# A fused attention and MLP kernel: q and k turned by VectorE in 32x32 blocks in place of DMA transposes, from the eighth group on

## The chip, the cores and the metric

One Trainium2 chip, of which the kernel uses one core. The metric is device time in microseconds (us), lower is better. The kernel before the change takes 414.19 us, the median of three runs (412.75 to 414.78). One of its executions was profiled; where a duration stands below, it comes from that execution. Engines are named as the profile names them: PE is TensorE's matmul, PEld its weight load, DVE is VectorE, ACT is ScalarE, POOL is GpSimd, and SP is SyncE, which here only issues DMAs.

## The reference

An attention over 8 batches of 12 heads, 448 rows of 64 columns each, with q and k normed by their root mean square, is followed by a two-layer MLP with a leaky activation:

```python
def rmsnorm(x, g):
    rms = np.sqrt(np.mean(x * x, axis=-1, keepdims=True) + 1e-06)
    return x / rms * g
q_n, k_n = (rmsnorm(q, g_q), rmsnorm(k, g_k))
scores = (1.0 / np.sqrt(64)) * np.matmul(q_n, k_n.transpose(0, 1, 3, 2))
scores = scores - np.max(scores, axis=-1, keepdims=True)
attn = np.exp(scores)
attn = attn / (np.sum(attn, axis=-1, keepdims=True) + 1e-09)
attn_out = np.matmul(attn, v)                      # (8, 12, 448, 64)

x = attn_out.transpose(0, 2, 1, 3).reshape(8 * 448, 12 * 64)
h = x @ w_in                                       # (3584, 768) @ (768, 2048)
g = np.maximum(h, 0.0) + alpha * np.minimum(h, 0.0)
out = g @ w_out                                    # (3584, 2048) @ (2048, 768)
```

## The kernel before

**Groups and bursts.** The work on q and k goes in 24 groups `y` of four heads, three groups to a batch. `TD` is 7: groups 0 to 6 are prepared in one way, groups 7 to 23, "from the eighth on", in another; it is the second way that the change replaces. A group has seven tiles `j` of keys. The program is a list of 69 bursts `n`. A burst issues two to four score tiles (`score`, PE, L357) with their exponentials (`soft`, ACT, L371), sums and products with v where they are due, and then the MLP units planned for it: `up` (first layer, PE L496, then ACT L536, then DVE L540), `down` (second layer), or `quad_a`, `quad_b`, `quad_c` (the second layer of two token tiles in seven products of half size in place of eight, L623). Each engine works through its instructions in the order of the program, which is written out by hand and by a small planner; nothing is reordered later.

**Preparing a group y >= 7.** `load_qk` loads q and k in two DMAs from SP's queue (L126), 128 partitions by 896 values, two head-halves of 64 partitions each. POOL squares them (`square`, L177), DVE sums each row of 64 (`reduce`, L185), ACT takes the logarithm and then the exponential of -0.5 times it (`root`, L195 and L196), POOL multiplies the rows by the result and writes them as fp16 (`scale`, L205), two DMA transposes put the 64 columns of each head on the partitions (`turn_dma`, L304), and DVE multiplies k in place by the product of the two gains (`turn`, L315). The scores of the group then read `qT` and `kT`.

**Order and places.** `root_at[y]` is the burst that holds `root` and `scale` of group y, `turn_at[y]` the burst that holds the gain product; in between the DMA transposes run by themselves. The roots of groups 7 to 23 stand in bursts 17, 20, 22, 24, 28, 29, 32, 36, 37, 40, 44, 45, 48, 52, 53, 56, 60, and their gain products in bursts 19, 23, 25, 27, 31, 33, 35, 39, 41, 43, 47, 49, 51, 55, 57, 59, 63. Within a burst the order is: scores and the first exponentials, sums and products, `root` and `scale` (L1116 to L1128), `turn_dma`, the load of a later group (L1132), and then the units of the burst with other small work (`jobs`) handed out between them, one after every second `up`. So ACT's logarithm of a root stands in ACT's queue ahead of the first `up` of its burst.

**Banks.** PSUM has two banks for scores (`pss`), two for everything of the MLP and half of the products with v (`psf`, tag `mm`: `hT`, `op`, `qx`, `qz`, `qc`, `avb`, `dnb`), and one pair (`psa`, tag `acc`) that the sums `dn`, the products `av` and now and then a spare MLP unit (`hTa`, `opa`, `qza`) take in turn. An `up` needs 1.14 us of PE; its bank is free again when ACT L536 (0.63 us) and then DVE L540 (0.62 us) have read it.

**Buffers.** `nat` (what is loaded) has four, `qs` (scaled rows) two, that is one group, `qT` and `kT` three each, `rden` (denominators) two. Groups 2, 5 and 8 are loaded into a piece of `arena`, which holds mixed weights later.

Of the kernel before, what the change touches and what calls it, by code (L numbers as in the profile page):

```python
# [21 lines left out]
def kernel(  # L22
# [17 lines left out]
    J = S // 64  # L40
    HH = H // 2
# [70 lines left out]
    def load_qk(y, hold=False):  # L112
        b, i = divmod(y, G)
        for nm in "qk":
            if y in (2, 5, 8):
                t = lent(HB + "qk".index(nm) * NB4, NB4).rearrange(
                    "p (h j d) -> p h j d", h=2, j=J
                )
            else:
                t = ld.tile([128, 2, J, D], FP32, name="nat", tag="nat", bufs=4)  # L120
            if hold and nm == "q":

                nc.scalar.copy(out=t[:, 0, 0, 0:1], in_=expb)
            o = t.rearrange("p h j d -> p h (j d)")
            for h in range(2) if (y, nm) == (0, "q") else (slice(0, 2),):
                nc.sync.dma_start(out=o[:, h], in_=SRC[nm][b, :, ds(2 * i, 2)][:, h])  # L126
            nat[y, nm] = t

# [34 lines left out]
    def square(y, nm):  # L163
        src = nat[y, nm].rearrange("p h j d -> p (h j d)")
        if y % 2 and y < 3 * G + 1:
            sq = lent(HB + (2 + "qk".index(nm)) * NB4, NB4).rearrange("p (n d) -> p n d", d=D)
        else:
            sq = ld.tile([128, 2 * J, D], FP32, name="sq", tag="sq", bufs=2)
        sqf = sq.rearrange("p n d -> p (n d)")
        if (y, nm) == (1, "q"):  # L170
            nc.scalar.activation(out=sqf, in_=src, func=AF.Square)
        else:

            n = 2 if (y, nm) in ((2, "q"), (G, "k")) else 1
            for h in range(n):
                c = ts(h, 2 * J * D // n)
                nc.gpsimd.tensor_mul(out=sqf[:, c], in0=src[:, c], in1=src[:, c])  # L177
        sqs[y, nm] = sq

    def reduce(y, nm, heads=None):  # L180
        if y not in ss_t:
            ss_t[y] = ld.tile([128, 2, 2, J], FP32, name="ss", tag="ss", bufs=4)
        o = ss_t[y][:, "qk".index(nm)].rearrange("p h j -> p (h j)").unsqueeze(2)
        for c in [slice(0, 2 * J)] if heads is None else [ts(h, J) for h in heads]:
            nc.vector.tensor_reduce(  # L185
                out=o[:, c], in_=sqs[y, nm][:, c], axis=AXIS_X, op=ALU.add
            )

    def root(y, nms="qk"):
        n = len(nms)  # L190
        at = "qk".index(nms[0])
        if at == 0:
            rr_t[y] = ld.tile([128, 2, 2, J], FP32, name="rr", tag="rr", bufs=4)
        rr, ss = rr_t[y][:, ds(at, n)], ss_t[y][:, ds(at, n)]
        nc.scalar.activation(out=rr, in_=ss, func=AF.Ln, scale=1.0 / D, bias=RMS_EPS)  # L195
        nc.scalar.activation(out=rr, in_=rr, func=AF.Exp, scale=-0.5)  # L196

    def scale(y, nm):
        if y in (1, 3, 5):
# [15 lines left out]
    def part_square(nm, h, j, eng):  # L215
        if ("sq", nm) not in tops:
            tops["sq", nm] = ld.tile([128, 2 * J, D], FP32, name="sq", tag="sq", bufs=2)
        o = tops["sq", nm].rearrange("p (h j) d -> p h j d", h=2)[:, h, j]
# [6 lines left out]
    def part_reduce(nm, h, j):  # L225
        if 0 not in ss_t:
            ss_t[0] = ld.tile([128, 2, 2, J], FP32, name="ss", tag="ss", bufs=4)
        nc.vector.tensor_reduce(
            out=ss_t[0][:, "qk".index(nm), h, j].unsqueeze(3),
            in_=tops["sq", nm].rearrange("p (h j) d -> p h j d", h=2)[:, h, j],  # L230
# [3 lines left out]
    def part_root(nm, j):  # L234
        if 0 not in rr_t:
            rr_t[0] = ld.tile([128, 2, 2, J], FP32, name="rr", tag="rr", bufs=4)
# [23 lines left out]
    def part_copy(nm, j, eng):  # L260
        if (0, nm) not in qkT:
            qkT[0, nm] = att.tile([128, J, 2, 64], FP16, name=f"{nm}T", tag=f"{nm}T", bufs=3)
# [18 lines left out]
    def turn_one(y, nm):  # L281
# [6 lines left out]
        t = att.tile([128, J, 2, 64], FP16, name=f"{nm}T", tag=f"{nm}T", bufs=3)  # L288
# [12 lines left out]
    def turn_dma(y):  # L301
        for nm in "qk":
            t = att.tile([128, J, 2, 64], FP16, name=f"{nm}T", tag=f"{nm}T", bufs=3)
            nc.sync.dma_start(  # L304
                out=t.rearrange("p j g c -> p j (g c)"),
                in_=qs[y, nm].rearrange("p j h d -> p (j h d)"),
                transpose=True,
            )
            qkT[y, nm] = t

    def turn(y):
# [21 lines left out]
        for tp, nm in zip(tps, "qk"):  # L333
            t = att.tile([128, J, 2, 64], FP16, name=f"{nm}T", tag=f"{nm}T", bufs=3)
# [84 lines left out]
    def den_pre(ys):  # L419
        accs = [psf.tile([128, 512], FP32, name="dnb", tag="mm") for _ in range(2)]  # L420
        ones_over(accs, ys)
        r = att.tile([128, 2, S], FP32, name="rden", tag="rden")[:, :, : cols_of(ys)]
# [8 lines left out]
    def log(ys):  # L431
        n = cols_of(ys)
        r = att.tile([128, 2, S], FP32, name="rden", tag="rden")[:, :, :n]
# [120 lines left out]
    def down(tile, oh, jobs=(), spare=False):  # L554
# [10 lines left out]
        for f, a in jobs:  # L565
            if f is not turn:
                f(*a)
        o = result()
        nc.vector.tensor_copy(out=o, in_=op[:, :OH])
        for f, a in jobs:  # L570
            if f is turn:
                f(*a)
# [472 lines left out]
    for n in range(NB):  # L1045
# [70 lines left out]
        if n in roots:  # L1116
            y = roots[n]
            work = [(root, (y,)), (scale, (y, "q")), (scale, (y, "k"))]
# [10 lines left out]
            if y >= TD:  # L1129
                turn_dma(y)  # L1130
# [22 lines left out]
        if ups_first and n in dens and not lead:  # L1153
            for f, a in jobs.pop(n, ()):
                f(*a)
        turned = n in turns and gaps[n] and (turns[n] >= TD or turns[n] <= 2 * G)
# [73 lines left out]
```

## Time and profile before

| what | profile of before |
|---|---|
| the profiled execution, device time | 414.78 us |
| its span, first to last instruction | 413.0 us |
| bytes moved by DMA | 53.38 MB, 129 GB/s on average |
| DMA packets under 512 bytes | 34880 of 67330 |
| PE idle, 46 to 90 us | 1.92 us |
| PE idle, 90 to 165 us | 0.07 us |
| PE idle, 165 to 330 us | 2.01 us |
| PE idle, 330 to 413 us | 4.19 us |
| POOL waiting for a load before a square, 90 to 330 us | 25.3 us in 6 waits |
| POOL waiting for a DMA transpose to free `qs` | 4.3 us in 3 waits |
| mean granted TensorE clock | 0.995 |

The profiled execution lies 0.6 us above the median of the three runs. The busy share of an engine is the time in which it executed something, over the span. A wait is put down to what ended it. The idle times of PE are 44, 75, 165 and 83 us less PE's busy time in these four stretches; the first group that is changed is loaded at 46.6 us, and the last one's gain product is at 328 us, so the second to fourth rows from the end of that list frame the part of the run that the change touches.

### The profile page before, as it was taken

Reading aid. Unit: us, or ns where it says so; the run is one execution under the profiler, and the core shown is the slowest. Engines: PE = TensorE matmul, PEld = TensorE weight load, DVE = VectorE, ACT = ScalarE, POOL = GpSimd, SP = SyncE. Lnnn points to the kernel's source line nnn. Section 1 sums busy time; section 2 is a strip of 40 time slices with the busy share of each in tenths; the row PEclk is TensorE's granted clock in tenths of the full one; section 3 lists DMA queues with packets and bytes.
Section 4 is the critical chain, followed back from the end, with each engine's and each line's share of the span. In section 5 each row is a group of like instructions: output and inputs, shape, how many; then the busy total and the mean of one; then the engine's idle time right before and its main releaser. Section 6 shows DMA issues by size and latency. Waiting matters only on the chain.

```text
span 413.0 us, 11724 instructions
## 1 busy us (share of the span) xinstructions
PE 398.9 (97%) x5055; PEld 208.1 (50%) x5055; DVE 266.9 (65%) x420; ACT 257.3 (62%) x390; POOL 255.8 (62%) x184
## 2 busy tenths in 40 slices
PE   7889999899999999999999999999999999999996
PEld 3344445444456445554455445545555455645664
DVE  3876875476567388785688585958576755465322
ACT  5697787567846785557766786875657783135110
POOL 5599996589677969376373847484724407300870
PEclk9899999999999999999999999999999999999999
DMA  8999899957754894329861697279332700320143
GB/s 259 231 217 206 172 200 155 248 169 103 163 81 134 204 169 91 115 63 197 144 168 48 173 138 177 63 180 193 59 75 54 127 3 24 75 59 0 30 103 97
DMA packets 67330, 53.38 MB, mean 129 GB/s; under 512 B 34880, under 2 KB 66768, under 8 KB 67280
## 3 DMA queue, kind: packets, MB, share of 16 engines
q1 hardware_dynamic: 53344, 40.45, 40.5%
q0 software_dynamic: 13536, 11.81, 21.5%
q8 instruction: 39, 0.64, 0.7%
q10 hardware_dynamic: 400, 0.39, 0.3%
q14 instruction: 11, 0.09, 0.1%
HBM read 45.62 MB, written 11.01 MB: 137 GB/s over the span
## 4 chain that ended last, share of the span: by engine, by line
PE 49%; DVE 6%; ACT 0%; issue 0%; DVEq 0%
PE hT L496 14%; PE hTa L496 7%; PE qx L623 5%; PE sc L357 3%; PE oq L623 3%; PE qc L623 3%; PE qz L623 2%; PE av L382 2%; PE oqm L623 2%; PE avb L382 1%; PE dn L382 1%; PE oqa L623 1%; DVE ss L185 1%; DVE xT L481 1%; DVE kT L315 1%; PE qza L623 1%
## 5 line engine op out<-in xcount | busy, mean ns | idle before, releaser
L371 ACT ACTIVATE expT<-sc 128x896 f16<-128x896 f32 x168 | 147.8, 913 | 55.4 <-PE sc L357 55.0
L496 PE MATMUL hT<-xT,w_in_sb 128*128 128x448 f16 x546 | 113.7, 353 | 0.4 <-DVE gT L540 0.2
L496 PEld LDWEIGHTS <-w_in_sb 128*128 128x128 f16 x768 | 72.7, 98 | 74.8 <-issue 10.1
L540 DVE TENSOR_TENSOR gT<-hT,gT 128x448 f16<-128x448 f32 x91 | 56.6, 623 | 40.1 <-ACT gT L536 39.2
L205 POOL TENSOR_TENSOR qs<-nat,rr 128x896 f16<-128x896 f32 x36 | 60.9, 1713 | 33.4 <-issue 24.9
L536 ACT ACTIVATE gT<-hT,cols 128x448 f16<-128x448 f32 x90 | 56.9, 633 | 33.9 <-PE hT L496 33.7
L177 POOL TENSOR_TENSOR sq<-nat 128x896 f32<-128x896 f32 x32 | 53.1, 1681 | 38.0 <-DMA nat<-in_q_dram 25.3
L357 PE MATMUL sc<-qT,kT 64*32 64x448 f16 (+1 forms) x1092 | 53.3, 358 | 3.5 <-ACT expT L371 1.1
L623 PEld LDWEIGHTS <-gT 128*128 128x128 f16 x352 | 33.4, 98 | 26.0 <-issue 4.9
L496 PE MATMUL hTa<-xT,w_in_sb 128*128 128x448 f16 x210 | 45.4, 352 | 0.0
L185 DVE TENSOR_REDUCE ss<-sq 128x14 f32<-128x896 f32 (+1 forms) x37 | 38.3, 1052 | 0.6 <-POOL sq L177 0.6
L481 DVE TENSOR_TENSOR xT<-av,rden 64x448 f16<-64x448 f32 (+1 forms) x37 | 27.2, 734 | 13.5 <-PE av L382 5.5
L536 ACT ACTIVATE gT<-hTa,cols 128x448 f16<-128x448 f32 x35 | 22.2, 635 | 19.1 <-PE hTa L496 19.1
L540 DVE TENSOR_TENSOR gT<-hTa,gT 128x448 f16<-128x448 f32 x35 | 21.8, 624 | 17.7 <-ACT gT L536 17.6
L357 PEld LDWEIGHTS <-kT 64*32 64x32 f16 (+1 forms) x1092 | 15.6, 93 | 34.7 <-issue 29.3
L558 PE MATMUL op<-w_out_sb,gT 128*128 128x384 f16 x160 | 27.4, 326 | 0.0
L382 PEld LDWEIGHTS <-vt 64*32 64x32 f16 x1344 | 20.2, 92 | 14.1 <-issue 5.0
L611 POOL TENSOR_TENSOR gs<-gT 128x1024 f16<-128x1024 f16 x3 | 6.4, 2121 | 30.3 <-DVE gT L540 28.1
L558 PEld LDWEIGHTS <-gT 128*128 128x128 f16 x192 | 18.0, 98 | 13.5 <-issue 2.4
L382 PE MATMUL av<-expT,vt 64*32 64x448 f16 x896 | 24.3, 350 | 0.3 <-DVE osb L671 0.3
L619 POOL TENSOR_TENSOR gT<-gT 128x1024 f16<-128x1024 f16 x11 | 23.8, 2166 | 0.0
L623 PE MATMUL qx<-w_out_sb,gT 128*128 128x384 f16 x120 | 20.9, 326 | 0.0
(148 smaller groups left out, 494.1 us busy)
## 6 DMA issues: line engine op xcount, KB each, us to landing
out_dram<-osb SPq DMA_DIRECT2D x107, 96.0 KB, 2.8
nat<-in_k_dram SPq DMA_DIRECT2D x21, 448.0 KB, 5.4
nat<-in_q_dram SPq DMA_DIRECT2D x20, 448.0 KB, 4.9
vt<-in_v_dram POOLq DMA_DIRECT2D x8, 672.0 KB, 11.0
w_in_sb<-in_moe_w_in_dram POOLq DMA_DIRECT2D x24, 128.0 KB, 5.0
w_out_sb<-in_moe_w_out_dram POOLq DMA_DIRECT2D x4, 768.0 KB, 10.8
arena<-in_q_dram SPq DMA_DIRECT2D x3, 448.0 KB, 7.8
arena<-in_k_dram SPq DMA_DIRECT2D x3, 448.0 KB, 8.5
```

The costliest lines, as they stand in the source:

```text
L177: nc.gpsimd.tensor_mul(out=sqf[:, c], in0=src[:, c], in1=src[:, c])
L185: nc.vector.tensor_reduce(out=o[:, c], in_=sqs[y, nm][:, c], axis=AXIS_X, op=ALU.add)
L205: eng.tensor_mul(out=t.rearrange("p j h d -> p h j d"), in0=nat[y, nm], in1=rr_t[y][:, "qk".index(nm)].unsqueeze(3).broadcast_to((128, 2, ...
L357: nc.tensor.matmul(out=sc[ds(64 * g + m * c, m), par, :S].rearrange("p (j c) -> p j c", j=J), lhsT=kT[ds(64 * par, 64), j, g, ts(c, m)], r ...
L371: nc.scalar.activation(out=expT[y][:, j], in_=scs[y, j][:, :, :S], func=AF.Exp, scale=QK_SCALE, bias=EXP_BIAS,)
L382: nc.tensor.matmul(out=accs[g][ds(32 * n, 32), :S], lhsT=weights(g, y, par, c, j), rhs=expT[y][ds(64 * g, 64), j, par, :], start=(j == 0), ...
L481: nc.vector.tensor_mul(out=x, in0=av, in1=r)
L496: nc.tensor.matmul(out=hT[:, :S], lhsT=w_in_sb[:, block_of(g, i), ts(ft, 128)], rhs=xT[b][:, g, i, :], start=(i == 0 and g == 0), stop=(i ...
L536: nc.scalar.activation(out=g, in_=hT[:, :S], func=AF.Copy, scale=alpha_sb[:, ft : ft + 1])
L540: nc.vector.tensor_max(out=g, in0=hT[:, :S], in1=g)
L558: nc.tensor.matmul(out=op[:, :OH], lhsT=gT[:, ft, ts(tile % J, 128)], rhs=w_out_sb[:, ft, ts(oh, OH)], start=(ft == 0), stop=(ft == NF - 1),)
L623: nc.tensor.matmul(out=bank[:, c], lhsT=g[:, ft], rhs=v[:, ft, c], start=(first and ft == 0), stop=(ft == HF - 1), skip_group_check=True,)
```

## The change

For groups 7 to 23 each row of q and k is loaded twice: partition quarters 0 and 2 hold it from column 0 on, quarters 1 and 3 from column 32 on, 32 tokens times 14 rows and two heads in each quarter. A tile is then 128 x 28 slots of 64 values, of which the first 32 are used; the squares are written over the second 32. Four DMAs per tensor take the place of one. A row's 64 squares now lie in two quarters, so each quarter's sums are half sums: `fold` swaps them between neighbouring quarters by four copies and adds. `scale` writes the fp16 rows so that the values of two neighbouring rows lie side by side as one 4-byte word, and `flip` turns 32x32 blocks of such words on DVE straight into `qT` and `kT`. `turn_dma` is gone; the gain product stays. The buffers are cut to make room: `nat` is twice as wide, `sq` is gone, `qT` and `kT` have two instead of three, `rden` one instead of two, `ss` and `rr` three instead of four. In groups 0 to 6 only the places of the squares change.

A `flip` pair stands one burst ahead of the gain product, among the jobs. But `qs` holds one group, so where the next group's root comes in that same burst or earlier, the pair is issued right in front of that root. By the bursts given above that is so for the flips of groups 8, 9, 11, 12, 14, 15, 17, 18, 20 and 21; those of 7, 10, 13, 16, 19, 22 and 23 are jobs.

```diff
@@ def load_qk
-            if y in (2, 5, 8):
-                t = lent(HB + "qk".index(nm) * NB4, NB4).rearrange(
-                    "p (h j d) -> p h j d", h=2, j=J
-                )
+            n = "qk".index(nm)
+            if y == 8:
+                t = lent(HB + 2 * n * NB4, 2 * NB4)
+            elif y in (2, 5):
+                t = lent(HB + n * NB4, NB4)
             else:
-                t = ld.tile([128, 2, J, D], FP32, name="nat", tag="nat", bufs=4)
+                t = ld.tile([128, 4 * J * D], FP32, name="nat", tag="nat", bufs=4)
+            if y >= TD:
+                load_twice(y, nm, t.rearrange("p (g t d) -> p g t d", g=2, d=D))
+                continue
...
+    def load_twice(y, nm, t):
+        b, i = divmod(y, G)
+        n = 2 * J * D - HD
+        for par in range(2):
+            src = FULL[nm][b, ds(4 * i + 2 * par, 2)].rearrange(
+                "g (p t) d -> p g (t d)", p=32
+            )
+            for e in range(2):
+                nc.sync.dma_start(
+                    out=t[ds(64 * par + 32 * e, 32)].rearrange("p g t d -> p g (t d)")[:, :, :n],
+                    in_=src[:, :, ds(HD * e, n)],
+                )
+        nat[y, nm] = t.rearrange("p g t d -> p (g t) d")
@@ def square
+        if y >= TD:
+            t = nat[y, nm]
+            sqs[y, nm] = t[:, :, HD:]
+            nc.gpsimd.tensor_mul(out=sqs[y, nm], in0=t[:, :, :HD], in1=t[:, :, :HD])
+            return
...
@@ def reduce
+        if y >= TD:
+            nc.vector.tensor_reduce(
+                out=ss_t[y][:, "qk".index(nm)].rearrange("p g h j -> p (g h j)").unsqueeze(2),
+                in_=sqs[y, nm], axis=AXIS_X, op=ALU.add,
+            )
+            return
...
+    def fold(y):
+        o = ld.tile([128, 4 * 2 * J], FP32, name="sf", tag="sf", bufs=1)
+        ss = ss_t[y].rearrange("p n g h j -> p (n g h j)")
+        for n in range(4):
+            nc.vector.tensor_copy(out=o[ds(32 * (n ^ 1), 32)], in_=ss[ds(32 * n, 32)])
+        nc.vector.tensor_add(out=ss, in0=ss, in1=o)
@@ def root
+        if y >= TD:
+            fold(y)
@@ def scale
+        if y >= TD:
+            t = ld.tile([128, J, HD, 4], FP16, name="qs", tag="qs", bufs=2)
+            r = rr_t[y][:, "qk".index(nm)].rearrange("p g h j -> p (g h) j")
+            nc.gpsimd.tensor_mul(
+                out=t.rearrange("p j d n -> p n j d"),
+                in0=nat[y, nm][:, :, :HD].rearrange("p (n j) d -> p n j d", j=J),
+                in1=r.unsqueeze(3).broadcast_to((128, 4, J, HD)),
+            )
+            qs[y, nm] = t.rearrange("p j d n -> p (j d n)").bitcast(FP32)
+            return
@@
-    def turn_dma(y):
-        for nm in "qk":
-            t = att.tile([128, J, 2, 64], FP16, name=f"{nm}T", tag=f"{nm}T", bufs=3)
-            nc.sync.dma_start(
-                out=t.rearrange("p j g c -> p j (g c)"),
-                in_=qs[y, nm].rearrange("p j h d -> p (j h d)"),
-                transpose=True,
-            )
-            qkT[y, nm] = t
+    def flip(y, nm):
+        t = att.tile([128, J, 2, 64], FP16, name=f"{nm}T", tag=f"{nm}T", bufs=2)
+        nc.vector.transpose(
+            out=t.rearrange("p j g c -> p (j g c)").bitcast(FP32).rearrange(
+                "p (j g c) -> p j g c", j=J, g=2
+            ),
+            in_=qs[y, nm].rearrange("p (j d g) -> p j g d", j=J, g=2),
+        )
+        qkT[y, nm] = t
...
@@ def down
-            if f is not turn:
+            if f not in (turn, flip):
...
@@ the list of bursts
         if n in roots:
             y = roots[n]
+            for nm in "qk" if y > TD and (y - 1, "q") not in qkT else "":
+                flip(y - 1, nm)
             work = [(root, (y,)), (scale, (y, "q")), (scale, (y, "k"))]
...
-            if y >= TD:
-                turn_dma(y)
...
+        flips = [(flip, (turns[n + 1], nm)) for nm in "qk"] if turns.get(n + 1, 0) >= TD else []
+        if flips and flips[0][1] not in qkT:
+            jobs.setdefault(n, []).extend(flips)
```

## The prediction

> **What bounds the kernel now.** I read the busy times first, then four stretches, the waits of PE and POOL, the DMA issues, and last the order of time around the roots. From the page, the windows (columns: PE, PEld, DVE, ACT, POOL busy, granted clock, DMA share, GB/s) and the issues:
>
> ```profile
> PE 398.9 (97%) x5055; PEld 208.1 (50%) x5055; DVE 266.9 (65%) x420; ACT 257.3 (62%) x390; POOL 255.8 (62%) x184
> ...
> 90.00:165.00 75.00, 74.93 (x872) 38.35 (x878) 48.56 (x74) 51.59 (x80) 62.82 (x39) 1.00 0.63 129
> 165.00:330.00 165.00, 162.99 (x2351) 84.71 (x2336) 121.31 (x193) 114.15 (x171) 92.23 (x55) 1.00 0.65 124
> ...
> nat<-in_k_dram SPq DMA_DIRECT2D x21, 448.0 KB, 5.4
> ...
> kT<-qs SPq DMA_TRANSPOSE x17, 3.7
> ```
>
> PE is the bound, and has next to nothing left: between 90 and 330 us it idles 0.07 + 2.01 = 2.1 us, with 46 to 90 us 4.0 us. Its work is not changed, so the change can gain 4.0 us at most, and whatever makes PE wait is lost in full. The DMA transposes end in no wait of PE or DVE; the only wait put down to them is POOL's for `qs`, 4.3 us in all. DVE is the busiest helper: 121.3 of 165 us (74%) from 165 to 330 us.
>
> The order of time around root 19 (burst 48) shows what PE hangs on:
>
> ```profile
> 241.80 1.08 DVE L185 TENSOR_REDUCE ss<-sq 128x14 f32<-128x896 f32 x1
> ...
> 242.79 0.61 DVE L540 TENSOR_TENSOR gT<-hT,gT 128x448 f16<-128x448 f32 x1
> 243.06 0.23 ACT L195 ACTIVATE rr<-ss 128x28 f32<-128x28 f32 x1
> 243.27 1.30 PE L496 MATMUL hTa<-xT,w_in_sb 128*128 128x448 f16 x6
> 243.31 0.23 ACT L196 ACTIVATE rr<-rr 128x28 f32<-128x28 f32 x1
> 243.32 0.68 DVE L611 TENSOR_TENSOR arena<-gT 128x1024 f16<-128x1024 f16 x1
> 243.47 0.63 ACT L536 ACTIVATE gT<-hT,cols 128x448 f16<-128x448 f32 x1
> 244.00 0.91 ACT L371 ACTIVATE expT<-sc 128x896 f16<-128x896 f32 x1
> 244.04 0.69 DVE L612 TENSOR_TENSOR arena<-arena,gT 128x1024 f16<-128x1024 f16 x1
> ...
> 245.47 0.62 DVE L540 TENSOR_TENSOR gT<-hTa,gT 128x448 f16<-128x448 f32 x1 [0.20 <-ACT gT L536]
> ...
> 246.15 1.52 PE L382 MATMUL dn<-expT,ones 64*32 64x448 f16 x56
> ```
>
> The root's logarithm (L195) stands in ACT's queue in front of the `up` reads (L536). They free the banks, and `dn` starts 0.06 us after DVE has freed hTa's pair. Now L195 needs only a reduce that is long done.
>
> **Removed.** 34 DMA transposes. SP no longer holds back loads behind them, and POOL's 4.3 us go. Neither is on PE's path: worth 0.
>
> **Added on DMA.** Each tensor grows from 458,752 bytes to 2 x 128 x 864 x 4 = 884,736, so a group moves 852 KB more. At the 231 to 259 GB/s of the first slices that is 3.3 to 3.7 us in a group's time of some 15 us (240 us for 16 groups), while DMA is 63 to 65% busy with the transposes in it. SP issues eight DMAs of 0.5 us for two of 0.5 and two of 1.2: 4 us for 3.5. Loads land some 3 us later after their issue but are issued 2 to 3 us sooner, right behind the scale that frees `nat`. Cover: square 18 starts at 217.3 us, on data landed at 216.6, and its reduces at 223.3. I take 0. Without cover POOL's squares are late, DVE stands in the reduce, and PE pays what is beyond some 2 us per group: 0 to 10 us in all.
>
> **POOL.** Squares and scales keep 896 elements a partition, with other strides. No row has such strides; the nearest are 1.64 us (768 fp16) to 2.17 us (1024 fp16). I take today's 1.68 and 1.71, the same count. At 2.17 the flips of 11, 17 and 20 come 2 x 0.46 later: 3 us.
>
> **DVE, per group.** A flip reads and writes 448 words of 4 bytes. A two-input product costs 620 ns at 448 and 1089 at 896 (1.05 ns per element); the row with 448 is the nearest: 0.62. Bounds: 0.55 (768 fp16 values, L591) and 1.09 (should a word go as two). Fold: four copies of 32x56 and an add of 128x56. The 128x32 memset takes 85 ns and the product of one column 161, so 4 x 0.10 + 0.2 = 0.6; bounds 0.4 (five of 85) and 0.9 (five of 177, the copy of 18 columns). A flip pair and a fold make 1.84 us (1.5 to 3.1), over 17 groups 31 us on DVE's 267.
>
> **Where it hurts: the wait that is new.** In ten groups (8, 9, 11, 12, 14, 15, 17, 18, 20, 21) the flips go right in front of the next root, and fold behind them. So L195 now waits for all of DVE's queue up to the fold, flips included, and these wait for POOL's scale. Behind L195 stand the burst's first L536, its exponential and the next L536; PE waits for their banks. The walk, each time with the times of before:
> - 18/19 (above): DVE is done with L612 at 244.73; flips and fold end at 246.57, where L195 starts, against 243.06. Then 0.5 root, 0.63, 0.91, 0.63 on ACT: hTa is read at 249.25, freed at 249.9. `dn` loses 3.8.
> - 20/21: fold 20 stands behind the muls of 265.5 and moves L195 from 266.28 to 267.35, the scales to 268.0 to 271.4. The second flip ends at 272.0, the fold at 272.6, where L195 21 was at 268.43; the first bank is free at 274.4, and the fourth `up` wants it at 271.3. 3.1, with the next one 3.2.
> - 17/18, the same: scale 17 until 231.1, fold 18 until 232.4 for 228.58, bank at 234.15 for 231.4: 2.8. 11/12: fold 11 behind muls until 134.3, scale until 138.2, L195 at 139.5 for 136.66: 2.0.
> - 9/10: L195 from 106.90 to 109.1, hTa free at 112.4 for 109.99: 2.4. 12/13, behind a DVE mix: 2.0. 8/9: 1.1. 15/16: 1.0.
> - 14/15 and 21/22, where products with their own banks come first: 0.6 and 0.3.
>
> Sum: 3.8 + 3.2 + 2.8 + 2.0 + 2.4 + 2.0 + 1.1 + 1.0 + 0.9 = 19.2. The seven other flip pairs and folds of bursts without such a pair are 7 x 1.84 = 12.9 us of DVE, covered by DVE's idle 43.7 us (165 to 330); I charge 1.5, and all 12.9 is the price without it. `turn` keeps its place 5 us behind, so a late flip delays no score. The cut buffers cost 0: with two `qT`, a flip waits for scores two groups back, which end before it in each case above; `rden` is rewritten after its products.
>
> 20.7 in all. The walks start each time from times of before, while a PE that has waited 3 us leaves the other engines ahead for the next place; I keep three quarters, 15.5. Against the profiled execution's 414.8 that is 430.3; the median of before lies 0.6 lower, so **430 us**. Own range, 0.4 to 1.5 of the sum: 422 to 445.
>
> **Rivals.**
> - **Absorbed (0.22).** Each of the ten has one more `up` of cover than I count (a third bank, 1.14 us): 19.2 - 10 x 1.1 = 8, so 422. For: at 198 to 200 us gains and reduces of over 3 us cost PE 0.13 us. Against: L195 holds ACT, not only DVE.
> - **Dearer (0.16).** Flips of 1.09 and folds of 0.9 add 1.24 at ten places (12 us), scales of 2.17 another 3: 445. For: no row shows a turn or such strides. Or late loads, up to 10.
> - **Turned into slack (0.06).** POOL and ACT give the 1.84 us back everywhere: 415. Against: DVE goes to 74% + 31/240 = 87%.
> - **Faster (0.05).** The one mechanism: keys are turned sooner and DMA is relieved, so that the waits of PE vanish. It would have to take back over half of PE's 4.0 us of idle between 46 and 330 us: 414.2 - 3 = 411. It decides only if a burst waited for a turned key now; k's gain product starts 5 to 18 us after its transpose landed. [...]
> - That the change doesn't do what it says: in ten of 17 groups the flip is not a burst ahead, as its list of jobs says, but at the root. That is in the code, and in my sum.
>
> **How the numbers follow.** Forecast 0.51. The range takes in "absorbed" and "dearer" and leaves out "slack" and "faster" and a far end: 417 to 446. What this measurement can tell from no change is about 0.5%, 2.1 us: faster 0.05; within 0.06; slower 0.89, from the first three cases.
>
> **What will show it.** PE's busy time stays at 399 and its idle between 90 and 330 us grows from 2.1 to some 15 us, in ten lumps of 0.3 to 4 us at the roots named, the largest at 19, 21 and 18. ACT's L195 gets waits for DVE's add in `fold`. DVE's busy time is near 298, a flip near 0.62, a fold near 0.6. POOL's two groups stay near 1.7. It is wrong if PE's idle stays below 5 us, if the lumps stand behind loads and squares, or if they stand where jobs flip.

## The result, and the profile after

The changed kernel takes 479.03 us (median of 4 runs, 478.12 to 481.3) where the kernel before takes 414.35 on the same chip (412.75 to 414.78). The ratio is 1.158, with a 95% interval of 1.153 to 1.163: 64.7 us slower. The prediction said 430 and at most 446.

The profiled execution took 478.5 us, its span is 476.7. From its page, the busy times and the clock that PE was granted in 40 slices:

```profile
PE 418.6 (88%) x5055; PEld 212.1 (44%) x5055; DVE 311.9 (65%) x539; ACT 258.1 (54%) x390; POOL 269.1 (56%) x184
...
PEclk9999999877989979998989999799899999999999
```

PE executes the same 5055 matmuls, but is busy 418.6 us instead of 398.9, and idle 476.7 - 418.6 = 58.1 us instead of 14.1. So the span's 63.7 us split in two: 44.0 us in which PE waits, and 19.7 us in which it computes more slowly. The second part is the clock: within the span the trace grants PE half its clock for 47.8 us in nine places (4.5 us before), in stretches of 3.4 or 6.8 us, each of which begins during a wait of PE or within 1.4 us of its end.

The stretches that the prediction read (PE, PEld, DVE, ACT, POOL busy, granted clock, DMA share, GB/s):

```profile
46.00:90.00 44.00, 39.12 (x535) 19.39 (x534) 26.43 (x43) 28.16 (x42) 30.38 (x21) 0.96 1.17 224
90.00:165.00 75.00, 61.91 (x638) 29.57 (x635) 49.70 (x80) 33.57 (x51) 47.43 (x29) 0.86 0.50 111
165.00:330.00 165.00, 139.11 (x1872) 69.14 (x1872) 120.31 (x218) 93.85 (x141) 91.01 (x50) 0.94 0.58 129
```

PE's idle time from 90 to 330 us has gone from 2.1 to 13.1 + 25.9 = 39.0 us, and the clock is lowest where the idle time is densest. Who waits for whom, and what the new instructions cost (waits: us in total, times, longest; groups: us, mean ns):

```profile
POOL qs L248 <- ACT rr L242: 75.0, 15, 15.2
...
ACT rr L241 <- DVE ss L229: 56.0, 16, 6.8
...
PE hT L550 <- DVE gT L594: 21.0, 7, 5.7
...
PE sc L411 <- ACT expT L425: 10.0, 4, 5.6
...
PE op L612 <- DMA w_out_sb<-in_moe_w_out_dram: 4.0, 1, 4.0
```

```profile
L248 POOL TENSOR_TENSOR qs<-nat,rr 128x896 f16<-128x896 f32 x32 | 67.6, 2205 | 79.3 <-ACT rr L242 73.8 <-issue 4.1 <-DVE ss L229 1.4
L194 POOL TENSOR_TENSOR nat<-nat 128x896 f32<-128x896 f32 x32 | 53.4, 1682 | 26.0 <-DMA nat<-in_k_dram 15.6 <-DMA nat<-in_q_dram 10.2
L228 DVE COPY sf<-ss 32x56 f32<-32x56 f32 x68 | 27.8, 409 | 1.1
L357 DVE STREAM_TRANSPOSE qT<-qs 128x448 f32<-128x448 f32 x17 | 10.8, 636 | 2.5 <-POOL qs L248 2.5
L357 DVE STREAM_TRANSPOSE kT<-qs 128x448 f32<-128x448 f32 x17 | 10.4, 614 | 4.4 <-POOL qs L248 4.4
```

The predicted wait is there: the root's logarithm (L241, L195 before) waits for the fold's add in 16 of 17 groups, 56 us in all, and GpSimd's scale waits behind it. The flip is as predicted (0.62 us). The fold's copy is not: 409 ns on average for 0.10. The mean hides two kinds: 56 copies take 0.18 us, twelve take 0.5 to 2.06. The order of time around root 8 shows three of the twelve (start, duration, engine, instruction):

```profile
92.38 1.68 POOL L194 TENSOR_TENSOR nat<-nat 128x896 f32<-128x896 f32 x1 [2.24 <-DMA nat<-in_k_dram]
92.44 5.04 DVE L228 COPY sf<-ss 32x56 f32<-32x56 f32 x4
...
94.02 3.22 POOL L645 TENSOR_TENSOR arena<-w_out_sb 128x768 f16<-128x768 f16 x2
94.34 1.30 PE L550 MATMUL hTa<-xT,w_in_sb 128*128 128x448 f16 x6
97.52 0.22 DVE L229 TENSOR_TENSOR ss<-ss,sf 128x56 f32<-128x56 f32 x1
...
97.83 0.25 ACT L241 ACTIVATE rr<-ss 128x56 f32<-128x56 f32 x1 [6.81 <-DVE ss L229]
...
98.27 0.90 ACT L425 ACTIVATE expT<-sc 128x896 f16<-128x896 f32 x1
...
99.45 4.64 PE L550 MATMUL hT<-xT,w_in_sb 128*128 128x448 f16 x12 [3.81 <-DVE osb L623]
```

GpSimd runs three instructions in a row here, 92.38 to 94.06 and 94.02 to 97.24, and VectorE's four copies take 5.04 us beside them: each long copy ends just behind the GpSimd instruction that ran beside it (the twelve end 0.04 to 0.05 us behind such an end, and none of the 56 short ones lies within a GpSimd instruction). PE has no free bank from 95.6 on and waits 3.8 us. At this root no flip stands in front.

### The profile page after: what moved, and what is told of

Read it like the earlier page. It is cut to its first block, busy times and chain, and to the rows that moved or that the text cites. A ratio compares the mean times of both kernels' runs of the same rounds, so it can differ in the third digit from the quotient of the medians.

```text
span 476.7 us, 11984 instructions
## 1 busy us (share of the span) xinstructions
PE 418.6 (88%) x5055; PEld 212.1 (44%) x5055; DVE 311.9 (65%) x539; ACT 258.1 (54%) x390; POOL 269.1 (56%) x184
## 4 chain that ended last, share of the span: by engine, by line
PE 36%; DVE 10%; DMA 3%; POOL 2%; ACT 2%; issue 1%; SPq 0%; DVEq 0%; ACTq 0%
PE hT L550 10%; PE qx L677 5%; PE hTa L550 5%; PE oq L677 3%; PE sc L411 2%; PE qz L677 2%; DVE sf L228 2%; POOL qs L248 2%; DVE ss L213 2%; PE oqm L677 2%; PE dn L436 2%; PE qc L677 1%; DMA nat<-in_k_dram 1%; PE av L436 1%; DMA nat<-in_q_dram 1%; DVE xT L535 1%
## 5 line engine op out<-in xcount | busy, mean ns | idle before, releaser
L550 PE MATMUL hT<-xT,w_in_sb 128*128 128x448 f16 x546 | 122.0, 369 | 26.8 <-DVE gT L594 21.0
L550 PEld LDWEIGHTS <-w_in_sb 128*128 128x128 f16 x768 | 75.0, 100 | 109.6 <-issue 49.6
L248 POOL TENSOR_TENSOR qs<-nat,rr 128x896 f16<-128x896 f32 x32 | 67.6, 2205 | 79.3 <-ACT rr L242 73.8
L194 POOL TENSOR_TENSOR nat<-nat 128x896 f32<-128x896 f32 x32 | 53.4, 1682 | 26.0 <-DMA nat<-in_k_dram 15.6
L411 PE MATMUL sc<-qT,kT 64*32 64x448 f16 (+1 forms) x1092 | 55.9, 375 | 12.6 <-ACT expT L425 10.0
L550 PE MATMUL hTa<-xT,w_in_sb 128*128 128x448 f16 x210 | 47.4, 363 | 0.0
L241 ACT ACTIVATE rr<-ss 128x56 f32<-128x56 f32 (+1 forms) x23 | 5.6, 243 | 57.4 <-DVE ss L229 56.0
L213 DVE TENSOR_REDUCE ss<-nat 128x28 f32<-128x896 f32 x32 | 33.9, 1076 | 0.0
L612 PE MATMUL op<-w_out_sb,gT 128*128 128x384 f16 x160 | 29.6, 343 | 4.0 <-DMA w_out_sb<-in_moe_w_out_dram 4.0
L228 DVE COPY sf<-ss 32x56 f32<-32x56 f32 x68 | 27.8, 409 | 1.1
L612 PEld LDWEIGHTS <-gT 128*128 128x128 f16 x192 | 18.6, 101 | 19.1 <-issue 8.7
L436 PEld LDWEIGHTS <-vt 64*32 64x32 f16 x1344 | 20.0, 92 | 14.1 <-issue 4.8
L673 POOL TENSOR_TENSOR gT<-gT 128x1024 f16<-128x1024 f16 x11 | 23.9, 2171 | 0.4 <-DVE arena L665 0.4
```

Source lines behind the costliest of these rows:

```text
L194: nc.gpsimd.tensor_mul(out=sqs[y, nm], in0=t[:, :, :HD], in1=t[:, :, :HD])
L213: nc.vector.tensor_reduce(out=ss_t[y][:, "qk".index(nm)].rearrange("p g h j -> p (g h j)").unsqueeze(2), in_=sqs[y, nm], axis=AXIS_X, op=A ...
L228: nc.vector.tensor_copy(out=o[ds(32 * (n ^ 1), 32)], in_=ss[ds(32 * n, 32)])
L248: nc.gpsimd.tensor_mul(out=t.rearrange("p j d n -> p n j d"), in0=nat[y, nm][:, :, :HD].rearrange("p (n j) d -> p n j d", j=J), in1=r.unsq ...
L411: nc.tensor.matmul(out=sc[ds(64 * g + m * c, m), par, :S].rearrange("p (j c) -> p j c", j=J), lhsT=kT[ds(64 * par, 64), j, g, ts(c, m)], r ...
L436: nc.tensor.matmul(out=accs[g][ds(32 * n, 32), :S], lhsT=weights(g, y, par, c, j), rhs=expT[y][ds(64 * g, 64), j, par, :], start=(j == 0), ...
```

## The experiments

Two theories stood against each other at first, for the 49 us that the forecast missed. A: the fold's copies wait for GpSimd, and everything else is as predicted. B: the copy is dear because it crosses the partition quarters. Behind both lay the question whether the fold's place, VectorE's plain load or the doubled loads do the rest. Each ratio below is against the kernel before on the same chip, with its 95% interval.

### The fold's copies

**unit.** The four copies become sums over an axis of length one, the same values by another instruction:

```diff
-            nc.vector.tensor_copy(out=o[ds(32 * (n ^ 1), 32)], in_=ss[ds(32 * n, 32)])
+            nc.vector.tensor_reduce(
+                out=o[ds(32 * (n ^ 1), 32)].unsqueeze(2), in_=ss[ds(32 * n, 32)].unsqueeze(2),
+                axis=AXIS_X, op=ALU.add,
+            )
```

> The changed kernel with the four swaps of each fold written as a sum over an axis of length one instead of as a copy; the values are the same. Theory A: a copy of 4-byte values from SBUF to SBUF on VectorE has to wait until the GpSimd instruction under way is done, and a sum does not. Then all 68 swaps take 0.1 to 0.2 us (the 56 short copies took 0.18), none over 0.3; VectorE's busy time falls from 312 to about 295 us, PE's idle time by 15 us or more, and the kernel comes to about 455 us. Theory B: it is the move to another partition quarter that is slow now and then. Then nothing changes: a mean of 0.4 us for a swap, a dozen over 0.5, and 479 us.

465.56 us, ratio 1.124 (1.118 to 1.130): 13 us less than the changed kernel, not the 24 expected. The groups show why:

```profile
L228 DVE TENSOR_REDUCE sf<-ss 32x56 f32<-32x56 f32 x68 | 13.7, 202 | 1.1
L232 DVE TENSOR_TENSOR ss<-ss,sf 128x56 f32<-128x56 f32 x17 | 9.9, 580 | 0.6
```

All 68 swaps take 198 to 207 ns, but the add, 0.22 us in every group of the changed kernel, now takes up to 1.60: it has taken over the wait in seven groups.

**same.** The copies stay in their own quarter (`n` for `n ^ 1`), so that each half sum is doubled instead of joined to its other half.

> The changed kernel with the fold's copies left in their own quarter, so that each half sum is doubled instead of completed (another value, the same work). Theory A (the copy waits for GpSimd's instruction): copies as before, a mean near 0.4 us, about a dozen over 0.5 us, 479 us. Theory B (the move between quarters is slow): all copies at or under 0.2 us, and about 455 us.

477.52 us, 1.152 (1.145 to 1.158), copies 410 ns on average and twelve long ones. Theory B falls.

**unit_sum.** unit, with the add also a sum, over pairs that lie in one tile. Where the next group's sums are formed ahead of a group's fold, the fold takes those, so some rows are scaled by another group's sums.

```diff
-        nc.vector.tensor_add(out=ss, in0=ss, in1=o)
+        nc.vector.tensor_reduce(
+            out=rr_t[y].rearrange("p n g h j -> p (n g h j)").unsqueeze(2),
+            in_=o.rearrange("p w c -> p c w"), axis=AXIS_X, op=ALU.add,
+        )
```

> unit with the fold's add also written as a sum (over pairs, unit axis kept), the halves and the swapped halves lying in one tile; same work, same order. In unit seven of the 17 adds took 0.28 to 1.60 us instead of 0.22, 6.2 us in sum, each ending 0.07 us before the GpSimd instruction that ran beside it. Theory (whichever instruction of the fold that is a copy or an add of two SBUF operands waits for the GpSimd instruction under way; in unit the add took over the wait that the copies had): no fold instruction above 0.3 us, the logarithm's waits for VectorE from 48.8 to some 42 us, time from 466 to 452 to 461 us. Rival (the adds' waits lay beside other work): adds as short, time 463 to 469.

No instruction of the fold is above 0.28 us any more (the swaps take 0.20 us on average, the add as a sum 0.27). The time is 462.4 us, 1.118 (1.110 to 1.125): just above what the theory gave, and its interval overlaps unit's. Theory A holds for the instructions; the copies' waits are worth about 13 us, and the adds' perhaps 2 more.

Why a copy or an add of two SBUF operands waits for GpSimd and a sum does not, no run shows. That it is so, the traces show in all three kernels: copies took up to 2.06 us in the changed kernel for 0.18 alone, adds up to 1.60 in unit for 0.22, the fold's sums never more than 0.28. The prediction had priced the fold without such a wait.

### The fold's place

**late.** Only the order changes: fold and logarithm first, the flips behind them, then the scale.

```diff
-            for nm in "qk" if y > TD and (y - 1, "q") not in qkT else "":
-                flip(y - 1, nm)
+            if y > TD and (y - 1, "q") not in qkT:
+                work[1:1] = [(flip, (y - 1, nm)) for nm in "qk"]
```

> The changed kernel with only the order turned at the ten roots where flips stand in front: fold and ScalarE's logarithm first, then the two flips of the group before, then the scale. Theory of the wait at the root: ScalarE's logarithm waits 1.25 us less at ten roots and no longer for GpSimd's scale at four (1.5 to 3 us each): its waits for the fold fall from 56 to about 35 us, PE's idle from 58 to about 40, and some of the half clock goes: 450 to 462 us. Rival: the flips only change places, VectorE's reads of the banks wait behind them instead, and PE waits as long: 474 to 481 us.

465.33 us, 1.126 (1.120 to 1.133), between the two. The logarithm's waits for the fold fall only from 56.0 to 46.5 us. The flips in front, on which the prediction put its weight, are thus the smaller part of what the logarithm waits for, though not cleanly priced: the copies wait longer for GpSimd here, 36.0 us in all for 27.8. One of them takes 4.97 us, beside three GpSimd instructions in a row.

**early.** unit, with the fold right behind k's sums instead of at the root, so that ten flip pairs still stand in front of the roots but the logarithm doesn't wait for them.

```diff
@@ def reduce
+            if nm == "k":
+                fold(y)
@@ def root
-        if y >= TD:
-            fold(y)
```

> The swaps as sums, as in the run 'unit', and the fold moved from the root to right behind the group's second reduce, some 2 to 10 us earlier; the flips stay in front of the root. Theory of the wait at the root: ScalarE's logarithm then waits for nothing but a fold that is done, so its waits for VectorE fall from 49 to under 8 us although every instruction is still there; PE's idle falls from 45 to 15 to 20 us (4 of them the wait for the second layer's weights near 81 us), the half clock from 29 to about 10 us, and the kernel comes to 425 to 438 us. Rival, the sheer load of VectorE: its 320 us of work are the same, the banks are read as late, and the time stays over 455 us.

442.13 us, 1.069 (1.065 to 1.073): 23 us less than unit, and 4 us above the theory's range. The logarithm's waits for the fold, 48.8 us in unit, are all but gone:

```profile
ACT rr L244 <- DVE ss L234: 4.0, 4, 1.3
```

VectorE does the same work as in unit; only the fold's place in its queue, and with it who waits for the fold, is different. What is left shows as a second kind of wait, in the order of time around 93 us:

```profile
93.09 1.09 DVE L213 TENSOR_REDUCE ss<-nat 128x28 f32<-128x896 f32 x1 [1.01 <-POOL nat L194]
93.47 0.63 ACT L593 ACTIVATE gT<-hT,cols 128x448 f16<-128x448 f32 x1 [0.50 <-PE hT L553]
94.22 0.85 DVE L230 TENSOR_REDUCE sf<-ss 32x56 f32<-32x56 f32 x4
95.10 1.22 DVE L234 TENSOR_TENSOR ss<-ss,sf 128x56 f32<-128x56 f32 x1
...
96.24 0.61 DVE L597 TENSOR_TENSOR gT<-hT,gT 128x448 f16<-128x448 f32 x1
96.77 0.61 DVE L597 TENSOR_TENSOR gT<-hTa,gT 128x448 f16<-128x448 f32 x1
96.90 1.29 PE L553 MATMUL hT<-xT,w_in_sb 128*128 128x448 f16 x6 [3.47 <-DVE gT L597]
```

Sums, swaps and add make a block of 3.2 us in VectorE's queue. The products that free the banks (L597) stand behind it, and PE waits 3.47 us.

**early_sum.** early with unit_sum's add.

> early with the same add as a sum. In early four of the 17 adds took 0.52 to 1.23 us, 2.9 us above the rest, and PE's longest lump (3.47 us at 93.2) stands behind one. Theory as for unit_sum: 436 to 440 us for early's 442.1, the lump at 93 down to some 2.4 us. Rival (what is left of early is load on VectorE and DMA, not these waits): 441 to 445.

443.0 us, 1.072 (1.067 to 1.077): the rival's. The adds' 2.9 us lay beside other work.

### What a late logarithm costs by itself

**pause_up, pause_down.** The kernel before, with one to five idle sums on VectorE in front of five roots, and a last sum that makes the logarithm wait for them; pause_down has them in the opposite order.

```diff
+        for _ in range({10: 1, 13: 2, 16: 3, 19: 4, 22: 5}.get(y, 0)):
+            nc.vector.tensor_reduce(
+                out=mark32, in_=w_in_sb[:, 0, :896], axis=AXIS_X, op=ALU.add
+            )
```

> The kernel before with nothing of the change, but with 1, 2, 3, 4 and 5 idle sums of VectorE (0.95 us each) and one more that the logarithm waits for, at the roots of groups 10, 13, 16, 19 and 22. It prices a late logarithm by itself. Theory: PE waits about as long as the logarithm is late less 0.8 to 1 us of cover (0, 1, 2, 3, 4 us, some 10 us in all), and where PE waited 2.5 us or more the granted clock falls to half for 3 to 7 us after it, which adds another 1.5 to 3 us each: 425 to 430 us. Rival: PE's waits add up alone and the clock stays, 0.99 and 420 to 424 us; or the cover is larger, and 417.

> The same with 5, 4, 3, 2 and 1 sums at the roots of groups 10, 13, 16, 19 and 22, to part the length of the pause from the place. If the length decides, the long waits of PE and the half clock move to the first two places; if the place decides, they stay at the last two. Time as in 'pause_up', 420 to 430 us.

One run each: 434.62 and 435.16 us beside 413.31, so 15 idle sums of 1.08 us, 16.2 us at five roots, cost 21 and 22 us, above what was expected. Five sums in front of root 10, in pause_down:

```profile
105.19 5.56 DVE L196 TENSOR_REDUCE mark<-w_in_sb 128x1 f32<-128x896 f16 x5
...
110.94 0.23 ACT L202 ACTIVATE rr<-ss 128x28 f32<-128x28 f32 x1 [5.91 <-DVE ss L201]
...
111.33 0.62 ACT L543 ACTIVATE gT<-hT,cols 128x448 f16<-128x448 f32 x1
111.85 0.91 ACT L378 ACTIVATE expT<-sc 128x896 f16<-128x896 f32 x1
...
112.81 0.59 PE L364 MATMUL sc<-qT,kT 64*64 64x448 f16 x4 [4.92 <-ACT expT L378]
```

This is the prediction's chain by itself: the logarithm is 5.9 us late, ACT's reads and exponential behind it too, and PE waits 4.9 us. Five sums in front of root 22 instead cost PE 3.1 us, one sum there nothing. At the nine places where the logarithm was late, by 1.4 to 6.0 us, PE waited 0.6 to 1.6 us less than it. So the mechanism was right. How late the logarithm is depends on the place too: two sums held it up by 4.4 us at root 13 and 3.8 at root 19, five by 5.9 at root 10 and 4.6 at root 22.

### The loads

**b_load2.** The kernel before, with each load of q and k from group 7 on issued once more, into spare device memory.

```diff
+            if y >= TD:
+                nc.sync.dma_start(
+                    out=spare_dram["qk".index(nm), y], in_=SRC[nm][b, :, ds(2 * i, 2)]
+                )
```

> The kernel before with each load of q and k from group 7 on issued a second time, into unused device memory, so that about as many more bytes are moved on the same queue as in the changed kernel; nothing waits for the second ones. Theory that the doubled bytes are hidden but for the early weights: 414 to 420 us, with at most one wait of PE of about 4 us for the second layer's weights near 80 us. Rival, the loads are a bound of their own: GpSimd waits longer for its squares, and 425 us or more.

423.64 us, 1.022 (1.016 to 1.029): 9.5 us, between the two. GpSimd's squares wait longer for their rows, 40.0 us in 14 waits for 25.3 in 6 before. It is not the price of the changed kernel's loads: with the transposes kept and the second rows written back to device memory, this kernel moves 69.0 MB, the changed one 60.1, the one before 53.4. In the changed kernel the doubled rows arrive in another form:

```profile
nat<-in_q_dram SPq DMA_DIRECT2D x64, 216.0 KB, 4.7
nat<-in_k_dram SPq DMA_DIRECT2D x64, 216.0 KB, 6.8
```

A quarter's 216 KB (third column) take k 6.8 us from issue to landing, where 448 KB took 5.4 before. What makes it slower is not shown: the partitions, the number of transfers and the length of their rows all differ from before, and no run here changed one of them alone.

### VectorE's work with nobody waiting for it

**dve_load.** The kernel before with sums of the size of early's flips and fold, on which nothing waits.

```diff
@@ def reduce
+        if y >= TD and nm == "k":
+            idle_sums((64, 64, 64, 64, 64))
@@ def root
+        if y >= TD:
+            idle_sums((512, 512))
```

> The kernel before with VectorE work of the size of early's flips and fold and nothing that waits for it: in each of the 17 groups two sums of 512 elements in front of the root (each near 0.6 us) and five of 64 behind k's reduce (each near 0.15 to 0.2). Theory (VectorE's plain load is a good part of early's 28 us, because it delays the gT products that free the banks): 422 to 430 us, PE idle from 14 to over 19 us. Rival (the load is hidden in VectorE's idle time): 413 to 418.

437.61 us, 1.058 (1.053 to 1.064): 24.8 us, more than either theory's number. Page and groups:

```profile
PE 405.1 (93%) x5055; PEld 209.8 (48%) x5055; DVE 299.9 (69%) x539; ACT 257.6 (59%) x390; POOL 255.6 (59%) x184
```

```profile
L182 DVE TENSOR_REDUCE mark<-w_in_sb 128x1 f32<-128x512 f16 x34 | 23.2, 683 | 0.8
L182 DVE TENSOR_REDUCE mark<-w_in_sb 128x1 f32<-128x64 f16 x85 | 18.5, 218 | 2.3
```

These 41.7 us stand in for early's 21.2 + 13.7 + 6.6 = 41.5 us of flips, swaps and adds. On an engine that was busy 65% of the time they cost more than half of themselves: PE's idle time goes from 14.1 to 31.7 us, and its busy time up by 6.2 with the clock.

**dve_and_loads.** The same on top of b_load2.

> b_load2 (each load of q and k issued twice) with the same VectorE work. If loads and VectorE's load together make early's time: 434 to 442 us. If they only add: b_load2's +9.5 and dve_load's own. If it stays below 430, the rest of early lies in the wait for the scaled rows (a scale of 2.2 us for 1.7, and flips that wait for it).

441.04 us, 1.064 (1.058 to 1.071): early's time, within the intervals. Loads and VectorE's load don't add up (24.8 + 9.5 would be 34, measured are 28.2): on top of VectorE's load the second loads cost 3.4 us, with intervals that overlap.

**dve_pairs, dve_pieces, dve_tail.** Two sums of 512 at the root only; one sum of 64 behind the release of each bank; all seven sums in one block behind k's gain product.

```diff
@@ def up, dve_pieces
             nc.vector.tensor_max(out=g, in0=hT[:, :S], in1=g)
+        if b > 0:
+            idle_sums((64,))
@@ def turn, dve_tail
+            idle_sums((512, 512, 64, 64, 64, 64, 64))
```

> The kernel before with two sums of 512 in front of each of the 17 roots (23 us in all), and nothing else of dve_load. If the cost goes by the sum of VectorE's work (dve_load: 24.8 us for 41.7): 424 to 430 us. If by blocks of over a microsecond that fall between the reading and the release of a bank, these are the larger of dve_load's two blocks: 428 to 434.

> The kernel before with one sum of 64 (0.22 us) behind the release of each bank in the bursts from the second batch of tokens on, 112 of them, 24 us in all: the same sum as dve_pairs, in pieces. If the cost goes by the sum: 424 to 430 us, as dve_pairs. If by the grain, the pieces lie in the 0.6 us that VectorE waits for ACT in front of most releases: 412 to 418.

> dve_load's whole work (two sums of 512, five of 64) in one block behind k's gain product, where the changed kernel's early flips go, and not at the roots. If the place at the root is what costs: below 425 us. If the sum or the block does: 433 to 442, as dve_load.

| kernel | VectorE work added | largest block, us | time, us | ratio (95%) |
|---|---|---|---|---|
| dve_pieces | 112 x 0.209 = 23.4 us | 0.2 | 413.5 | 1.002 (0.999 to 1.005) |
| dve_pairs | 34 x 0.683 = 23.2 us | 1.4 | 419.07 | 1.015 (1.012 to 1.019) |
| dve_load | 41.7 us in two blocks per group | 1.4, and 1.1 behind a sum of 1.08 | 437.61 | 1.058 (1.053 to 1.064) |
| dve_tail | 42.0 us in one block per group | 2.5 | 451.54 | 1.094 (1.091 to 1.098) |

(The blocks are the sums of the means in the groups; 5 x 0.22 = 1.1, 2 x 0.686 + 5 x 0.22 = 2.5.) The same 23 us cost nothing measurable in pieces behind the releases, as the second theory had it, and 6 us in pairs, below both numbers expected of the pairs. The same 42 us cost 25 in two blocks and 38 in one, above what either theory gave. So it isn't the sum. Block and place were changed together in these kernels, and they don't tell one from the other.

### Attempts at a better changed kernel

**early_scale.** early with GpSimd's scale writing its values one behind the other.

> early with GpSimd's scale writing its fp16 values one behind the other instead of 8 bytes apart (the pairs that the flip turns are then other columns, so q and k come out with their columns mixed: the output differs). The scale should go from 2.2 to near 1.7 us, 17 us less GpSimd time. If the flips' wait for it is a part of early's 442: 434 to 439. If it lies beside other work: 440 to 444.

The scale falls to 1.71 us, the time is 441.9, 1.070 (1.067 to 1.074): the 0.5 us more of each scale lay beside other work.

**spread, cut, cut2.** early with flips, scale and load moved behind two or three `up` products of their burst; in cut and cut2 each flip is also cut into four.

```diff
+                    root(y)
+                    parts = [(y - 1, nm, c) for nm in "qk" for c in CUTS]
+                    late += [(1 + 3 * i // 8, flip, a) for i, a in enumerate(parts)]
+                    late += [(3, f, a) for f, a in work[1:]]
```

> As 'early', and in the bursts of three or more first-layer units the two flips, the scale and the load behind it are issued after the second unit instead of ahead of the first. If, with the fold early, what is left at the roots is VectorE standing in a flip that waits for GpSimd's scale (6.7 us in 'unit', four roots) and 1.25 us of flips ahead of the first bank read, this is 3 to 8 us faster than 'early'. If instead the scales come too late by it, flips and gain products move onto the path, and it is as slow or slower.

> spread (445.3 us: early with the root's flips, scale and load behind two up products) with every flip cut into four, two columns of batches at a time (each near 0.2 us), and spread over the bank releases of three up products where the burst has them (nine of the ten roots; scale and load behind the third), and one piece per up product in the seven other groups. Fold and reduce stay one block. If blocks cost and not the sum: 432 to 439 us. If what is left is loads, scales that start later and the block of reduce and fold: 441 to 448, as spread.

> cut with each flip done once: 130 pieces for the 34 flips. In cut a piece of 128 words took 0.27 to 0.29 us and one of 64 0.21, so a flip in four is about 1.05 us instead of 0.62: some 14 us more VectorE time in all than in early, 12 less than in cut. If blocks cost and not the sum: 430 to 438 us. If what is left lies elsewhere, or the pieces' own overhead takes the gain: 440 to 448.

445.26 us, 1.077 (1.072 to 1.083); 451.3, 1.091 (1.086 to 1.096); and 446.96, 1.082 (1.076 to 1.087). In spread and cut six groups' flips ran twice, seen in spread's groups:

```profile
L360 DVE STREAM_TRANSPOSE qT<-qs 128x448 f32<-128x448 f32 x23 | 14.6, 634 | 0.0
L360 DVE STREAM_TRANSPOSE kT<-qs 128x448 f32<-128x448 f32 x23 | 14.0, 610 | 0.0
```

23 for 17, so these two say nothing on the move. In cut2 each runs once, but two sevenths of a flip (128 of 448 words) take nearly half as long as a whole one:

```profile
L365 DVE STREAM_TRANSPOSE kT<-qs 128x128 f32<-128x128 f32 x48 | 11.4, 274 | 0.0
L365 DVE STREAM_TRANSPOSE qT<-qs 128x128 f32<-128x128 f32 x48 | 11.2, 282 | 0.0
...
L365 DVE STREAM_TRANSPOSE qT<-qs 128x64 f32<-128x64 f32 x16 | 3.5, 220 | 0.0
L365 DVE STREAM_TRANSPOSE kT<-qs 128x64 f32<-128x64 f32 x16 | 3.3, 204 | 0.0
```

The pieces and the two whole flips left take 29.4 + 1.2 = 30.6 us where early's flips took 21.2, and nothing is gained. Whether smaller blocks without that price would help the changed kernel stays open. No version came near the kernel before.

## Why the prediction was wrong

The direction was right, and so was the chain on which it was built: a late fold, a late logarithm, banks freed late, PE waiting. Its sum was far too small. Three terms failed: the fold, put at 0.6 us and measured at 1.85; PE's busy time, put at no change and 19.7 us longer; and the cover of the other flips and folds. In the changed kernel's trace PE waits 30.9 us at the ten roots of the walk, where 19.2 were walked, and 15.5 were forecast in all. The other 13.1 of its 44.0 us of added idle time lie elsewhere.

The experiments cut the time another way. Differences of the kernels' excess over the kernel before, each on its own chip, lay out the 64.7 us:

| step | us |
|---|---|
| VectorE's work alone, nobody waiting (dve_load) | 24.8 |
| loads on top, and what else early has (early, 28.8) | 4.0 |
| the fold at the root, with the logarithm behind it (unit, 51.4, less early) | 22.6 |
| the fold's copies waiting for GpSimd (64.7 less unit) | 13.3 |

The rows hold in this order. The first stands for the changed kernel's own work only as far as dve_load's sums stand where that work does: the same sums cost 38 us in dve_tail. The clock is inside each row: a halved clock costs half of its duration while PE computes, 47.8 / 2 = 23.9 us in the changed kernel against 2.2 before, which roughly agrees with the 19.7 us by which PE's busy time grew. (In the changed kernel's trace the 128x448 products of the first layer follow each other at 0.19 us at full clock and at 0.37 at half.)

By its steps:

- **"Fold: four copies ... 4 x 0.10 + 0.2 = 0.6; bounds 0.4 and 0.9": failed.** It took 4 x 0.409 + 0.217 = 1.85 us, over the upper bound. A copy by itself took 0.18; the rest is the wait for GpSimd. The profile of before had shown such a wait, and the prediction did not use it. VectorE's add and difference at L611 and L612, with both operands in SBUF, take 0.68 and 0.69 us alone; beside GpSimd's scales they took 1.59 to 2.06, at 157 us and again here:

```profile
206.13 3.78 POOL L205 TENSOR_TENSOR qs<-nat,rr 128x896 f16<-128x896 f32 x2
206.44 1.93 DVE L611 TENSOR_TENSOR arena<-gT 128x1024 f16<-128x1024 f16 x1
...
208.41 2.06 DVE L612 TENSOR_TENSOR arena<-arena,gT 128x1024 f16<-128x1024 f16 x1
```

- **The ten roots, 19.2 us: mechanism and most places right, size off by the fold.** With 1.85 for 0.6 the walk would have given 19.2 + 10 x 1.25 = 31.7; the lumps of PE's idle time at these ten roots sum to 30.9. The largest are at 12 (5.7 us), 19 (5.6), 21 and 18 (3.8 each); 19, 21 and 18 were named, 12 was walked at 2.0. Roots 15 and 22, walked at 0.6 and 0.3, show none. Keeping three quarters of the sum was wrong: the later places didn't recover.
- **"The seven other flip pairs and folds ... covered by DVE's idle 43.7 us; I charge 1.5": failed.** At roots 8 and 14, where no flip stands in front, the fold with its long copies alone is followed by PE waits of 3.8 and 2.4 us. And dve_load shows that work of the size of all flips and folds costs 24.8 us with no new wait on the logarithm. Of VectorE's 70.1 us of idle time between 90 and 330 us before, 39.4 are 64 short waits for ACT, none over 1.9. Such gaps hid pieces of 0.2 us (dve_pieces) and not blocks of one or two; that it is the block and not its place is likely, but not shown.
- **PE's busy time "stays at 399": failed.** No term of the sum had the clock, and the 19.7 us are more than the whole forecast loss.
- **Loads "I take 0", bounds 0 to 10:** the heavier loads of b_load2 cost 9.5 alone, but 3.4 on top of VectorE's load. In the changed kernel one PE wait of 4.0 us is for the late `w_out` weights, a neighbour that the sum did not look at.
- **POOL "at 1.71", bound 2.17:** the scale took 2.2, just over the bound, the square 1.68. In early the longer scale was worth nothing (early_scale).
- **Flip 0.62: right. Removed transposes worth 0:** nothing speaks against it, and no run tests it alone. The same holds for the cut buffers at 0: early, which has them, takes as long as dve_and_loads, which hasn't, within the intervals.
- **The rivals.** "Dearer" (445) had the right sign, mostly for a wrong reason, flips of 1.09. "Absorbed", "faster" and "slack" failed.

## What to carry to other kernels

Price an added VectorE instruction by what may run on GpSimd beside it: here a short copy (0.18 us alone, up to 2.06 beside GpSimd) or an add of two SBUF operands (0.22 alone, up to 1.60) took until the GpSimd instruction under way had ended, once until the third in a row had (4.97 us, in late), and a sum over an axis of one did the copy's work without that wait, in 0.20. Where PE is full and its banks are freed by VectorE, do not count idle time of VectorE as cover by its sum: here it covered pieces as short as its gaps, and longer blocks only in part, so look at the gaps one by one. And count a longer wait of PE with half of the slow stretch that can follow it: in the changed kernel nine of the ten waits of 2.4 us or more were followed by 3.4 or 6.8 us at half the clock.

## What was not expected of the hardware

The clock falls for 3.4 us or twice that, and the length of the wait alone doesn't say when. In dve_load a wait of 1.81 us (from 237.6) left it whole, one of 1.90 (258.5) was followed by 3.4 us at half; in the changed kernel one of 2.42 (214.4) halved it, one of 3.77 (273.8) did not. All changes of the clock in a trace lie on one grid, wherever the waits lie: in the changed kernel's trace the 19 changes are whole multiples of 3.413 us apart, and so are the three in that of before.

The grid also sorts the waits. That of 3.77 us falls on two slots of the grid, 1.82 us of idle time in one and 1.95 in the next; those of 1.90 and 2.42 lie whole in one. In the 20 traces of this case, each of the 80 slots at full clock in which PE idled 1.96 us or more was followed by one at half, none of the 2329 with less than 1.4 us was, and of the 68 in between ten were. In the traces of before and after alone these are nine of nine, none of 226, and one of six. A slot at half in the changed kernel was followed by a second in the five cases in which PE idled 0.78 to 2.60 us in it, which makes the stretches of 6.8 us, and by full clock in the nine in which it idled 0.40 us or less.
